# Keys turned before the query maxima, a ninth weight buffer, and maxima subtracted four chunks at a time

## The chip, the cores and the metric

The kernel runs on one core of one Trainium2 chip. A time is the device time of one execution in microseconds (us). The kernel before took 442.67 us, the median of three runs (442.42 to 442.70). The profile is of one further execution, which took 442.15 us. The profiler's span of that execution, from its first to its last instruction, is 440.3 us; the other 1.9 us lie around it.

## The reference

Two layers follow one another. The first is a linear attention with softmax-like features ("hedgehog"), for 8 batches, 8 heads, 576 positions and 64 channels a head:

```python
def phi(x):
    proj = np.einsum('bhsd,df->bhsf', x, w_phi)              # 64 -> 128 features
    proj = proj - np.max(np.abs(proj), axis=-1, keepdims=True)
    return np.concatenate([np.exp(proj), np.exp(-proj)], axis=-1)
q_p, k_p = (phi(q), phi(k))
kv = np.einsum('bhsf,bhsd->bhfd', k_p, v);  z = np.sum(k_p, axis=2)
x = np.einsum('bhsf,bhfd->bhsd', q_p, kv) / (np.einsum('bhsf,bhf->bhs', q_p, z)[..., None] + 1e-06)
```

The second takes x as (8, 576, 512), transforms it over the positions, mixes the channels of the first 64 frequencies, each with a complex 512x512 matrix of its own (w_r, w_i), transforms back and ends with a small channel layer:

```python
X = np.fft.rfft(x, axis=1)[:, :64]
Yr = Xr @ w_r[m] - Xi @ w_i[m];  Yi = Xr @ w_i[m] + Xi @ w_r[m]      # for each frequency m
u = x + np.fft.irfft(Y, n=576, axis=1)
out = u + np.maximum(u @ w_ch, 0.0)
```

The frequency matrices are 64 x 512 x 512 x 2 numbers in float32, 134 MB of the 163.6 MB that the core reads.

## The kernel before, in words

**Attention.** The work is cut into 16 units, each of two batches and two heads (`Unit`, four groups g of heads by four pairs bp of batches). A unit goes through stages that are spread over four turns of one loop (lines 490 to 557): in turn n, unit n+2 (called R) has its keys and queries turned by TensorE (`turn_k`, `turn_q`), unit n+1 (K) gets its maxima and the exponentials of its keys (`rows_k`, `rows_q`, `exp_k`), unit n (Q) gets the sums over keys, the query features and the result (`kv`, `cols_q`, `exp_q`, `num`), and unit n-1 (P) is transformed over positions (`freq`, `keep_x`).

The maximum over features must be subtracted from the query features. The query features are laid out with features in partitions and positions in columns, while the maxima are found in the other layout (`rows_q`, a VectorE reduce). So `shift_q` (line 214) splits each maximum into three bf16 parts (two VectorE subtracts), TensorE transposes them into `pt`, ScalarE copies that to `mT` (96 x 128), and `cols_q` (line 229) subtracts them inside the accumulation: after each product of 512 columns, `shifted` adds four products of 128 columns whose weights are one column of `minus`, broadcast; each picks the maxima of one chunk of 128 positions.

**Mixing.** The frequency matrices come as 64 transfers of 8 frequencies, a quarter of the input channels and one of the two parts, read as 2 MB of float32 and cast to 1 MB of bf16 on the way (`wload`). `mix` takes one of them in 8 products. Each group of four units adds its 16 (or 12) matrices to the queue `mixq`; `some(n)` takes n of them in the attention loop, and each, unless it lay in borrowed memory (`held`), asks with `next_w(1)` for the next transfer. 44 matrices are mixed in the loop, the last 20 in the loop at line 884.

**After attention.** The loop at line 884 does between two mixes what else can be done: the channel layer of x alone, and the inverse transform of the frequencies that are complete (`todo`, `fill`). When the last matrix is mixed, the rest of the inverse transform, the last sum and the 20 stores of the output follow (`Last`, lines 940 to 966).

**Order and buffers.** Each engine keeps program order (`InOrder`). All loads of keys, queries, values and matrices are issued by GpSimd (POOL), one behind the other; a load that must wait for its buffer holds all behind it. Matrices have 8 buffers of 8 KB a partition (pool `pw`, tag "wt", line 83), keys, queries and values 2 each (`pin`). Tiles named `one` share four PSUM banks in rotation, tiles named `two` two pairs of banks. In the last part `yall` and `yl`, the frequencies brought together, take buffers of "wt" too, and so do output tiles (`of`, `ofr`, `rx`); `zall` has memory of its own in `pb` (line 575). All three are written by small copies that SyncE (SP) and POOL issue.

All calls go through the helper at line 37, so the profile gives L37 for nearly all instructions, and the tiles' names tell them apart.

Of the kernel before, what the change touches and what calls it, by code (L numbers as in the profile page):

```python
# [43 lines left out]
def kernel(  # L44
# [14 lines left out]
    pe, dve, act = (InOrder(tc, e) for e in (nc.tensor, nc.vector, nc.scalar))  # L59
# [20 lines left out]

    XTb = [pers.tile([128, 2, 2, 2, 2, B_, 32], BF16, name=f"XT{i}") for i in range(2)]

    pw_cm = tc.tile_pool(name="pw", bufs=8)
    pw = pw_cm.__enter__()
    pin_cm = tc.tile_pool(name="pin", bufs=2)
    pin = pin_cm.__enter__()
# [1 line left out]
    pm = pm_cm.__enter__()  # L88
    m3s = [pm.tile([128, 3, 32], F32, name=f"m3{i}", bufs=1) for i in range(2)]
    minus = pm.tile([96, 32], BF16, name="minus", bufs=1)  # L90


    def load(t, src, g, bp, eng):
# [6 lines left out]
    class Unit:  # L100
# [36 lines left out]

        def turn_q(self, part):
            if part == 0:
                self.qT = pm.tile([128, 9, 128], BF16, name="qT", bufs=3)  # L140
                self.m3 = m3s[self.bp % 2]
            self.turn(self.qb, self.qT, False, part)

# [70 lines left out]
        def shift_q(self):  # L214

            high = self.m3.bitcast(BF16).rearrange("p t (n s) -> p t n s", s=2)[:, :, :, 1]
            for t in range(2):
                dve.tensor_tensor(out=self.m3[:, t + 1, 0:18], in0=self.m3[:, t, 0:18],
                                  in1=high[:, t, 0:18], op=ALU.subtract)
            pt = one([96, 128], BF16)  # L220
            pe.transpose(pt, high.rearrange("p t n -> p (t n)"), ident_b)
            self.mT = pm.tile([96, 128], BF16, name="mT")
            act.copy(self.mT, pt)

        def shifted(self, out, n, stop):
            pe.matmul(out, lhsT=minus[:, n:n + 1].to_broadcast([96, 128]), rhs=self.mT,
                      start=False, stop=stop)

        def cols_q(self, i):

            if i < 2:
                ps = two([128, 2, 4, 128])
                for c2 in range(2):
                    pe.matmul(
                        ps[:, c2].rearrange("p n s -> p (n s)"),
                        lhsT=w2blk[:, c2 * 128:(c2 + 1) * 128],
                        rhs=self.qT[:, 4 * i:4 * i + 4, :].rearrange("p n s -> p (n s)"),
                        start=True, stop=False,
                    )
                    for j in range(4):  # L240
                        self.shifted(ps[:, c2, j, :], 8 * i + 2 * j + c2, j == 3)
            else:
                ps = one([128, 2, 128])
                for h in range(2):
                    pe.matmul(ps[:, h, :], lhsT=w2blk[:, h * 128:(h + 1) * 128],
                              rhs=self.qT[:, 8, :], start=True, stop=False)
                    self.shifted(ps[:, h, :], 16 + h, True)
            self.pa = ps

        def exp_q(self, i):  # L250
# [131 lines left out]
    ident_f = scr[:, 2176:2304]  # L382
# [9 lines left out]
    mf = scr[:, 2112:2176]  # L392
# [8 lines left out]
    def sc(i):  # L401
# [21 lines left out]
    for t in range(3):  # L423
        r = slice(32 * t, 32 * t + 32)
        dve.tensor_scalar_mul(out=minus[r], in0=ident_f[r, r], scalar1=-1.0)

    def forward_table():

# [58 lines left out]
    def unit(i):  # L487
        return units[i] if 0 <= i < len(units) else None

    for n in range(-2, len(units) + 1):  # L490
        P, Q, K, R = (unit(n + i) for i in (-1, 0, 1, 2))
        X = 0 if n < 4 else 6 if n == 4 else 3
        if Q:
            Q.exp_q(0)
        if K:
            K.rows_k(0)
            K.exp_k(0)
        if Q:
            Q.weigh_v2()
            if unit(n + 2):  # L500
                unit(n + 2).load_v()
        if P:
            P.freq()
            P.keep_x()
            if P.bp == NP - 1:
                mixq += [key for key in order if key[0] == P.g and (P.g < 2 or key[1] < 12)]
            if n == 4:
                some(2)
        if Q:
            Q.cols_q(1)  # L510
            Q.exp_q(1)
        some(1 if X else 0)
        if K:
            K.rows_k(1)
            K.exp_k(1)
        if Q:
            Q.kv()
        if K:
            K.rows_q(0)
            K.rows_k(2)  # L520
            K.rows_q(2)
            K.rows_q(1)
# [361 lines left out]
    while mixq:  # L884
        key = mixq.pop(0)
        g, o, i = key[0], key[1] // 2, key[1] % 2
# [9 lines left out]
        n = -(-max(len(todo) - A, 0) // (left - 7)) if left > 7 else math.ceil(len(todo) / (left - 0.4)) if left else 0  # L896
        if g == NG - 1 and i == 1:
# [5 lines left out]
            pt = [bank([128, 2, 128], BF16) for h in range(2)]  # L903
# [94 lines left out]
```

## Time and profile before

| | before |
|---|---|
| median of 3 runs | 442.67 us (442.42 to 442.70) |
| profiled execution, its span | 442.15 us, 440.3 us |
| busy, share of the span | PE 76%, DVE 65%, ACT 64%, POOL 22% |
| moved by DMA | 99.57 MB as written, mean 226 GB/s |
| `mT<-one` copy on ACT, x16 | 0.262 us each |
| `two<-mT,minus`, 128 columns, x256 | 0.219 us each (overlapping) |
| weight loads of `minus`, x288 | 0.098 us each |
| a transfer of a matrix | 18.4 us (w_r), 18.6 us (w_i) from issue to landing, median |

PE is TensorE, PEld its weight loads, DVE VectorE, ACT ScalarE. Busy shares are of the whole span, over parts with different limits: attention runs to about 300 us, mixing alone to about 404 us, and the output to the end. DMA's bytes are counted as written, after the cast. [...] the landing comes later, and how much later tells what lies ahead of it in the queue.

### The profile page before, as it was taken

What the parts mean: (1) busy time and instruction counts of PE and PEld (TensorE: products, weight loads), DVE (VectorE), ACT (ScalarE), POOL (GpSimd) and SP (SyncE); (2) the same over time, 40 slices, a digit from 0 to 9 for tenths busy, and PEclk for the clock granted to TensorE, in tenths of its full rate; (3) what the DMA queues carried; (4) which work ended last, traced back from release to release, by engine and by line L of the source; (5) the groups of instructions that cost most, each with busy time, mean ns of one, the idle gap of its engine ahead of it and who ended that gap; (6) DMA issues with size and microseconds to landing.
All of it is one profiled execution on the core that took longest, in us unless ns stands there. A gap on an engine that the chain in (4) does not pass through costs nothing.

```text
span 440.3 us, 10505 instructions
## 1 busy us (share of the span) xinstructions
PE 335.4 (76%) x4395; PEld 219.8 (50%) x4439; DVE 285.7 (65%) x560; ACT 282.6 (64%) x494; POOL 96.9 (22%) x138
## 2 busy tenths in 40 slices
PE   2577587577877867768778677597679998999993
PEld 2356475454655656556557556474335544343320
DVE  4655765864658556787596576768864334777694
ACT  3595786866869668778587577752544442656682
POOL 7132031111402122223123121124002121010071
PEclk9986886978969888989699689879999999999997
DMA  7999999999999999999999999999999999997787
GB/s 165 237 210 211 237 212 237 234 216 264 210 212 237 239 236 218 197 237 210 239 210 238 214 236 238 212 212 213 212 216 222 219 222 223 212 219 159 240 363 305
DMA packets 51583, 99.57 MB, mean 226 GB/s; under 512 B 2512, under 2 KB 13648, under 8 KB 51536
## 3 DMA queue, kind: packets, MB, share of 16 engines
q0 software_dynamic: 45376, 86.45, 99.9%
q1 hardware_dynamic: 6160, 12.45, 8.0%
q8 instruction: 34, 0.56, 0.5%
q14 instruction: 13, 0.11, 0.1%
HBM read 163.64 MB, written 9.44 MB: 393 GB/s over the span
## 4 chain that ended last, share of the span: by engine, by line
PE 41%; DVE 24%; ACT 17%; DMA 8%; issue 8%; POOL 1%; ACTq 0%; DVEq 0%; POOLq 0%
PE one L37 18%; PE pt L37 10%; ACT AB L37 9%; PE two L37 8%; DVE m L37 7%; DMA wt<-in_moe_w_r_dram 7%; DVE mk L37 6%; PE pp L37 4%; ACT XT L37 3%; DVE xs L37 2%; DVE XT L37 2%; ACT AQ L37 2%; DMA qb<-in_q_dram 2%; ACT kT L37 1%; DVE yacc L37 1%
## 5 line engine op out<-in xcount | busy, mean ns | idle before, releaser
L37 ACT ACTIVATE AB<-two 128x1024 bf16<-128x1024 f32 x64 | 62.0, 1026 | 13.1 <-DVE mk L37 9.2
L37 ACT ACTIVATE AQ<-two 128x1024 bf16<-128x1024 f32 x64 | 62.6, 1043 | 3.3 <-PE two L37 3.2
L37 ACT CAST xw<-pt 128x512 bf16<-128x512 f32 x50 | 29.4, 588 | 34.4 <-PE pt L37 34.4
L37 DVE TENSOR_REDUCE mk<-two 128x8 f32<-128x1024 f32 x32 | 38.9, 1218 | 15.1 <-PE two L37 15.1
L37 DVE RECIPROCAL rd<-one 128x6 f32<-128x6 f32 x48 | 9.4, 195 | 59.9 <-PE one L37 59.9
L37 DVE TENSOR_REDUCE m<-two 128x8 f32<-128x1024 f32 x32 | 39.2, 1224 | 12.8 <-PE two L37 12.6
L37 DVE TENSOR_TENSOR va<-vn,ee 128x1152 bf16<-128x1152 f32 x32 | 41.9, 1353 | 0.0
L37 PE MATMUL pt<-wchb,xT 128*128 128x512 bf16 x127 | 34.0, 379 | 9.3 <-DVE xT L37 7.7
L37 ACT COPY kT<-one 128x512 bf16<-128x512 bf16 (+1 forms) x32 | 19.3, 640 | 32.7 <-PE one L37 32.6
L37 PEld LDWEIGHTS <-xs 128*128 128x128 bf16 x624 | 31.3, 102 | 12.2 <-issue 6.8
L37 PEld LDWEIGHTS <-minus 96*128 96x128 bf16 x288 | 28.3, 117 | 17.2 <-issue 12.4
L37 POOL DMA_DIRECT2D wt<-in_moe_w_i_dram x28 | 20.9, 747 | 70.5 <-PE one L37 39.0
L37 POOL DMA_DIRECT2D wt<-in_moe_w_r_dram x30 | 22.3, 745 | 64.0 <-PE one L37 34.7
L37 PE MATMUL two<-w2blk,qT 128*128 128x256 bf16 x128 | 20.6, 286 | 19.5 <-ACT AB L37 9.6
L37 PE MATMUL two<-mT,minus 96*128 96x128 bf16 x256 | 31.3, 258 | 3.8 <-issue 2.8
L37 PEld LDWEIGHTS <-qT 128*128 128x128 bf16 x144 | 14.2, 101 | 37.0 <-issue 34.4
L37 POOL DMA_DIRECT2D kb<-in_k_dram x16 | 11.5, 718 | 89.7 <-PE one L37 88.9
L37 PE MATMUL one<-kvz,AQ 128*128 128x65 bf16 x512 | 31.1, 223 | 0.0
L37 PE MATMUL one<-wt,XT 128*32 128x512 bf16 x304 | 26.2, 434 | 4.6 <-DVE XT L37 2.7
L37 PEld LDWEIGHTS <-AQ 128*128 128x128 bf16 x512 | 27.9, 119 | 1.6 <-issue 0.4
L37 PE MATMUL two<-w2blk,kT 128*128 128x256 bf16 x128 | 21.7, 300 | 8.4 <-ACT AB L37 8.4
L37 DVE TENSOR_TENSOR xs<-one,rd 128x384 bf16<-128x384 f32 x48 | 26.7, 557 | 1.6
(144 smaller groups left out, 707.4 us busy)
## 6 DMA issues: line engine op xcount, KB each, us to landing
wt<-in_moe_w_r_dram POOLq DMA_DIRECT2D x30, 1024.0 KB, 18.4
wt<-in_moe_w_i_dram POOLq DMA_DIRECT2D x28, 1024.0 KB, 18.6
vn<-in_v_dram POOLq DMA_DIRECT2D x15, 576.0 KB, 13.3
out_dram<-of SPq DMA_DIRECT2D x16, 512.0 KB, 3.1
kb<-in_k_dram POOLq DMA_DIRECT2D x16, 288.0 KB, 12.4
qb<-in_q_dram POOLq DMA_DIRECT2D x16, 288.0 KB, 12.5
xs<-in_moe_w_i_dram POOLq DMA_DIRECT2D x2, 1024.0 KB, 22.6
yacc<-in_moe_w_r_dram POOLq DMA_DIRECT2D x1, 1024.0 KB, 9.6
```

Source lines behind the costliest of these rows:

```text
L37: ins = f(*args, **kwargs)
```

## The change

1. In the loop, `turn_k(0)` of unit R (four transposes of keys) is put ahead of `shift_q` of unit K, and `turn_k(1)` (five) right behind it. Both stood behind `cols_q(0)`. The load of the next keys stays where it was on POOL.
2. `shift_q` makes `mT` four times as wide: VectorE multiplies the transposed maxima, repeated four times, by a mask `apart`, so that block j keeps the rows of chunk j alone. `cols_q` then subtracts the maxima of four chunks in one product of 512 columns. The ScalarE copy goes. `apart` and new columns of `minus` are made at the start, by seven VectorE instructions.
3. The matrices get a ninth buffer, and after turn 3 one more transfer is asked for. `qT` has 2 buffers in place of 3, `mT` 1 in place of 2, and `zall` moves from its own memory into a buffer of "wt".
4. In turn 4 the two mixes `some(2)` move from behind `keep_x` to behind `kv`.

```diff
-    pw_cm = tc.tile_pool(name="pw", bufs=8)
+    pw_cm = tc.tile_pool(name="pw", bufs=9)
...
+    apart = pm.tile([96, 4], BF16, name="apart", bufs=1)
...
-                self.qT = pm.tile([128, 9, 128], BF16, name="qT", bufs=3)
+                self.qT = pm.tile([128, 9, 128], BF16, name="qT", bufs=2)
...
-            self.mT = pm.tile([96, 128], BF16, name="mT")
-            act.copy(self.mT, pt)
+            self.mT = pm.tile([96, 4, 128], BF16, name="mT", bufs=1)
+            dve.tensor_tensor(out=self.mT, in0=pt.unsqueeze(1).to_broadcast([96, 4, 128]),
+                              in1=apart.unsqueeze(2).to_broadcast([96, 4, 128]), op=ALU.mult)
...
-                    for j in range(4):
-                        self.shifted(ps[:, c2, j, :], 8 * i + 2 * j + c2, j == 3)
+                    self.shifted(ps[:, c2].rearrange("p n s -> p (n s)"), 2 * i + c2,
+                                 self.mT.rearrange("p j s -> p (j s)"))
...
+    every = mf[0:96, 0:32]
+    for t in range(3):
+        r = slice(32 * t, 32 * t + 32)
+        dve.tensor_copy(every[r], ident_f[r, r])
+    dve.tensor_reduce(out=mf[0:96, 32:36], in_=every[:, 0:32].rearrange("p (a j c) -> p j a c", a=4, j=4), axis=AX.XY, op=ALU.add)
+    dve.tensor_copy(apart, mf[0:96, 32:36])
+    dve.tensor_reduce(out=mf[0:96, 32:36].rearrange("p (a c) -> p a c", a=2), in_=every[:, 0:16].rearrange("p (a j c) -> p a c j", a=2, j=4), axis=AX.X, op=ALU.add)
+    dve.tensor_scalar_mul(out=minus[:, 0:4], in0=mf[0:96, 32:36], scalar1=-1.0)
...
-            if n == 4:
-                some(2)
...
+        some(2 if n == 4 else 0)
...
+        if R:
+            R.turn_k(0)
         if K:
             K.shift_q()
+        if R:
+            R.turn_k(1)
         if Q:
             Q.num(0)
         if K:
             K.cols_q(0)
-        if R:
-            R.turn_k(0)
-            R.turn_k(1)
-            if unit(n + 4):
-                unit(n + 4).load_k()
+        if R and unit(n + 4):
+            unit(n + 4).load_k()
...
+        elif n == 3:
+            next_w(1)
...
-    zall = pb.tile([128, B_, DMODEL], BF16, name="zall", bufs=1)
+    zall = pw.tile([128, B_, DMODEL], BF16, name="zall", tag="wt")
```

More of the change, by code (lines that the diff above doesn't have):

```diff
@@ L221, in shift_q, with shifted @@
             pe.transpose(pt, high.rearrange("p t n -> p (t n)"), ident_b)
-            self.mT = pm.tile([96, 128], BF16, name="mT")
-            act.copy(self.mT, pt)
-        def shifted(self, out, n, stop):
-            pe.matmul(out, lhsT=minus[:, n:n + 1].to_broadcast([96, 128]), rhs=self.mT,
-                      start=False, stop=stop)
+            self.mT = pm.tile([96, 4, 128], BF16, name="mT", bufs=1)
+            dve.tensor_tensor(out=self.mT, in0=pt.unsqueeze(1).to_broadcast([96, 4, 128]),
+                              in1=apart.unsqueeze(2).to_broadcast([96, 4, 128]), op=ALU.mult)
+        def shifted(self, out, n, rhs):
+            pe.matmul(out, lhsT=minus[:, n:n + 1].to_broadcast([96, 128]), rhs=rhs,
+                      start=False, stop=True)
         def cols_q(self, i):
@@ L246, in cols_q @@
                               rhs=self.qT[:, 8, :], start=True, stop=False)
-                    self.shifted(ps[:, h, :], 16 + h, True)
+                    self.shifted(ps[:, h, :], 16 + h, self.mT[:, 0, :])
             self.pa = ps
@@ L425 @@
         dve.tensor_scalar_mul(out=minus[r], in0=ident_f[r, r], scalar1=-1.0)
+    every = mf[0:96, 0:32]
+    for t in range(3):
+        r = slice(32 * t, 32 * t + 32)
+        dve.tensor_copy(every[r], ident_f[r, r])
+    dve.tensor_reduce(out=mf[0:96, 32:36],
+                      in_=every[:, 0:32].rearrange("p (a j c) -> p j a c", a=4, j=4),
+                      axis=AX.XY, op=ALU.add)
+    dve.tensor_copy(apart, mf[0:96, 32:36])
+    dve.tensor_reduce(out=mf[0:96, 32:36].rearrange("p (a c) -> p a c", a=2),
+                      in_=every[:, 0:16].rearrange("p (a j c) -> p a c j", a=2, j=4),
+                      axis=AX.X, op=ALU.add)
+    dve.tensor_scalar_mul(out=minus[:, 0:4], in0=mf[0:96, 32:36], scalar1=-1.0)
     def forward_table():
```

## The prediction

> **What bounds the kernel now.** I read the page's slices and queues first.
>
> ```profile
> span 440.3 us, 10505 instructions
> ...
> DMA  7999999999999999999999999999999999997787
> GB/s 165 237 210 211 237 212 237 234 216 264 210 212 237 239 236 218 197 237 210 239 210 238 214 236 238 212 212 213 212 216 222 219 222 223 212 219 159 240 363 305
> ...
> q0 software_dynamic: 45376, 86.45, 99.9%
> ```
>
> No engine is near 100%, but the DMA engines are over 90% in every slice from 11 to 396 us, and the packets of POOL's queue q0 fill 99.9% of sixteen engines' time (they overlap, so that sum alone proves little). The question is whether this is a full pipe or only a long wait in it. The DMA view of single issues, asked for short windows at 179, 302 and 369 us, decides (last column: us from issue to landing).
>
> ```profile
> wt<-in_moe_w_i_dram POOLq DMA_DIRECT2D x1, 1024.0 KB, 9.9
> ...
> wt<-in_moe_w_r_dram POOLq DMA_DIRECT2D x1, 1024.0 KB, 32.2
> wt<-in_moe_w_i_dram POOLq DMA_DIRECT2D x1, 1024.0 KB, 37.6
> ...
> wt<-in_moe_w_i_dram POOLq DMA_DIRECT2D x1, 1024.0 KB, 35.2
> ```
>
> With POOL's issue times these give landings. The matrices issued at 295.66, 297.94, 300.15 and 300.94 us land at 313.2, 318.0, 323.1 and 328.0: 4.95 us apart, whatever the distance of their issues. The last, issued at 369.06, lands at 404.3, after 35.2 us, 30 of them behind six others. So the matrices come as fast as the queue gives them, and one that is asked for earlier only stands in the queue longer.
>
> Then the timeline, for who waits for whom near the end (start, us, engine, operation; idle time in brackets).
>
> ```profile
> 368.09 0.20 PEld L37 LDWEIGHTS <-XT 128*32 128x32 bf16 x8 [0.89 <-DMA wt<-in_moe_w_r_dram]
> ...
> 404.56 0.66 PE L37 MATMUL pt<-wt,XT 128*32 128x512 bf16 x8
> ...
> 415.92 1.22 DVE L37 TENSOR_TENSOR of<-pp,rl 128x1024 f32<-128x1024 f32 x1 [0.48 <-DMA out_dram<-of]
> ```
>
> At 368 us TensorE waits for a matrix; from there on it works nearly without a gap and meets the last one 0.3 us after its landing. The two run abreast: DMA needs 36.2 us from 368.05 to 404.3, TensorE 36.5 from 368.09 to 404.56. The 36 us after that need the last matrix and are fixed. The chain of waits names PE 41% and DMA only 8%; it follows a load back to the mix that freed its buffer, and so hides that the queue itself is the limit.
>
> Before 300 us attention does not follow DMA: at 282.8 us TensorE mixes a matrix that landed 28 us earlier (issued at 236.9, 18.1 us to landing). Its last mix in the loop starts at 300.5 us, 2.4 us after its matrix landed (283.72 + 14.4 = 298.1). That 2.4 us is all that a faster attention can hand on.
>
> **What the Trainium skill says.** "DMA: Bandwidth & Descriptors", section "Where 436 GB/s comes from", puts the ceiling of a core's SBUF ports at 435 GB/s. A matrix reads 2.097 MB in 4.95 us: 424 GB/s, so the trace agrees and the pipe is full. The same page, "Issuing engines are not separate DMA queues", says that transfers of all issuers share 16 engines: between 328 and 368 us, where SP's copies of `yst` and `zst` run, matrices land 5.2 to 6.2 us apart. "VectorE: DVE Perf Modes", "The perf-mode tier table", gives `tensor_tensor` with a PSUM operand the plain rate; the rows here agree (128x512 in 0.69 us, 128x384 in 0.56).
>
> **Part by part.** *Keys ahead of the maxima.* One turn before (69 to 74 us):
>
> ```profile
> 69.93 0.34 PE L37 MATMUL one<-ident_b,m 128*96 128x128 bf16 x1 [1.51 <-DVE m L37]
> ...
> 70.31 0.26 ACT L37 COPY mT<-one 96x128 bf16<-96x128 bf16 x1 [0.46 <-PE one L37]
> ...
> 72.43 1.17 PE L37 MATMUL one<-ident_b,kb 128*128 128x128 bf16 x9
> ```
>
> Four of nine transposes, 4/9 x 1.17 = 0.52 us, fall into the wait of 1.51. But the banks of `one` rotate by four: in the turns with mixing (n from 4 on) the running sum of `mix` takes one, and `turn_k(0)` must wait for the bank that `exp_k(2)` reads. At 195 us that read ends at 195.94, while the maxima's transpose started at 195.47 after a wait of 0.26. There it starts 0.5 (bank) + 0.5 (four transposes) - 0.1 = about 0.9 us later, and what is moved forward is only given back behind it. So: +0.5 us a turn for the six early turns, 0 for the later (between -0.9 and +0.5). POOL: the load of keys can be issued up to 2 us earlier; that only lengthens its stay in the queue.
>
> *Wide mT.* VectorE gains 16 x about 0.65 us (between the 0.56 and 0.69 rows), ScalarE loses 16 x 0.262. `mT` is ready 0.4 us later, covered by `turn_k(1)` (0.65) and `num(0)` (0.87), which stand ahead of its reader; without this cover 0.4 a turn. TensorE: two groups of four 128-column products take 0.43 us each at 71 us, where a product of 512 columns takes 0.42: gain 0. At 61 us the eight take 0.83, where two of 512 would take 0.42: 0.4 gained, beside a wait for ScalarE. I take 0.4 a turn on the path, between 0 and 0.8. The start gets seven VectorE instructions (copies of 32x32 like the 0.17 of `minus`, small reduces), about 1.5 us, while the queue holds over 10 us of loads.
>
> Attention in sum: 6 x 0.5 + 16 x 0.4 - 1.5 = about +8 us, from -8 (6 x 0.5 - 11 x 0.9 - 1.5) to +14. Of a gain, 2.4 us reach the mixing loop, and there TensorE meets the DMA wait of 368 us earlier. At the end: 0.
>
> *Ninth buffer and the extra load.* Bytes, their order at the end and the stores are the same, so 404.3 moves only where the pipe ran thin. There is one such place; DMA's rate from 170 to 190 us in half-us slices:
>
> ```profile
> GB/s 213 204 213 205 208 208 203 175 171 230 283 359 249 280 177 174 160 184 139 147 201 201 205 217 168 205 184 197 217 221 201 213 213 217 228 190 200 199 207 207
> ```
>
> At 172.9 us the queue holds only 3.8 us of work (the loads before it land by 176.7). Against about 208: six slices from 177 us at a mean of 163.5 lose 0.64 us, two at 173.5 lose 0.17, four from 182 lose 0.19; together 1.0. The landings agree: 5.8 and 5.2 us for two matrices, 1.2 over. With one more matrix ahead the queue has 3.8 + 4.95 us there: gain 1.0, between 0.4 and 1.3. The extra load goes ahead of the values of unit 6, issued at 98.15 and landed after 9.9 us; with 5 more they use 15 of the 34 us until they are read. `some(2)` behind `kv` delays one matrix load by about 5 us, with 8 + 5 us of queue as cover.
>
> *Places.* `qT` with 2 and `mT` with 1: their last readers come before the writers in the same turn; 0. `zall` in "wt": in the mixing loop 9 - 2 buffers in place of 8 - 1 (`yl` is first written at 386 us, when all loads are issued); 0. It is free before the output, so there one more buffer stands ready, and the 0.48 us wait of `of` at 415.92 goes; TensorE ran half beside it: 0.2 gained (0 to 0.4).
>
> Sum: 1.0 + 0.2 = 1.2 us. The profiled execution would take 442.15 - 1.2 = 441.0; it is 0.5 below the median, so the median comes to 442.67 - 1.2 = 441.5.
>
> **Rivals.** *Nothing at all.* The thin place is one of many small losses, another arises, or the queue gets no deeper because the new loads wait elsewhere on POOL: 442.4 to 442.9. For it: other matrices land 0.3 to 0.8 us late in a full queue (118.6 us, 271.6). Against: the rate falls only where the queue is short.
>
> *Attention's gain comes through.* 8 us off: 434. For it: 25.6 us of TensorE's weight loads wait for the maxima. Against: TensorE would have to mix matrices before they land.
>
> *The bank of `exp_k(2)`.* In the eleven late turns the maxima come 0.9 us later and nothing is gained back: 10 us lost and 1.5 at the start, 3 gained early. Attention then ends 8 us late; TensorE has 0.9 us in hand at 368, so the end comes 7 us later: 449.8. It decides as soon as attention ends more than 0.9 us later than before. For it: the wait of 0.26 leaves no room. Against: four transposes fewer stand between the maxima and `num(6)`, and only the sum counts there.
>
> **How the numbers follow.** Pipe refilled 0.68 (440.6 to 442.3), nothing 0.16, gain through 0.03, bank 0.13 (443.6 to 452). A measurement can tell about 0.2% from no change: below 441.8 is faster, above 443.55 slower. Three quarters of the first case (0.51) and the third give faster 0.54; the rest of the first and the second give same 0.33; slower 0.13. The range leaves out the third case, the last and a few hundredths of the first: 440.3 to 443.6.
>
> **What would show it.** Right: the last matrix lands at about 403.3 us, the rate near 175 us stays above 200 GB/s, the wait of `of` is gone, 36 us follow the last mix, and attention ends earlier than 300.5 us with longer landings. Wrong: a last mix that starts well after its landing (attention or mixing became the bound), an empty q0, values landing after 32 us, or a tail that is not 36 us.

## The result, and the profile after

| | before | after |
|---|---|---|
| median | 442.69 us (442.42 to 443.00, 4 runs) | 442.92 us (441.78 to 443.16, 4 runs) |
| ratio of the two | | 1.0000 (95%: 0.9981 to 1.0019) |
| profiled execution, its span | 442.15 us, 440.3 us | 443.16 us, 441.4 us |
| last matrix lands | 404.27 us | 404.06 us |
| last mix starts | 404.56 us | 405.24 us |
| from there to the span's end | 35.7 us | 36.1 us |

With four executions on each side nothing is seen. Two later comparisons, with more executions, give 441.06 us against 441.87 (0.9988, 95%: 0.9978 to 0.9997) and 441.40 against 441.80 (0.9986, 0.9976 to 0.9995). The medians differ by 0.8 and 0.4 us, and both intervals leave out 1 (the ratios are the record's own and not the quotients of the medians). So there is a gain, of about 0.13%. The first comparison, uncertain by 0.19%, could not have shown it.

The page of the changed kernel, with the same rows as were shown of the one before:

```profile
span 441.4 us, 10119 instructions
...
DMA  8999999999999999999999999999999999995787
GB/s 164 237 211 210 237 212 237 235 214 242 233 211 238 223 230 232 237 216 233 232 216 235 208 236 231 219 212 211 211 216 223 221 224 215 213 218 127 243 354 305
...
q0 software_dynamic: 45376, 86.45, 99.6%
...
DMA 39%; PE 30%; DVE 12%; ACT 9%; issue 7%; POOL 0%; ACTq 0%; POOLq 0%; DVEq 0%
```

Slices and queue are as full as before. The one slice that was low, 197 GB/s in the 17th, reads 237. The chain of waits has turned round, DMA 39% where it was 8%, though the limit is the same. Attention now arrives early and waits for matrices, so the chain meets the transfers that it formerly passed by.

The rate in half-us slices from 170 to 190 us, asked of DMA as before:

```profile
GB/s 225 205 209 201 225 217 205 201 221 254 188 191 207 221 200 206 202 247 290 299 285 255 294 312 290 241 193 213 209 221 201 209 217 225 197 209 217 221 205 202
```

No slice is below 188, where eight were at or below 177 before. The thin place, the stretch in which the queue had little work left and the rate fell, is gone. The last matrix is issued at 369.95 us; the DMA view of that issue has it land 34.1 us later.

```profile
wt<-in_moe_w_i_dram POOLq DMA_DIRECT2D x1, 1024.0 KB, 34.1
```

So the pipe was refilled, and in this execution its end came 0.2 us sooner, not 1.0. From there to the last mix it took 0.9 us longer, and from the last mix to the end 0.4 us longer. The 0.4 are taken up with the single parts below; for the 0.9 TensorE's timeline tells where (start, us, engine, operation; idle time in brackets):

```profile
362.17 0.66 PE L37 MATMUL pt<-wt,XT 128*32 128x512 bf16 x8 [1.31 <-DMA wt<-in_moe_w_i_dram]
...
364.16 1.80 PE L37 MATMUL pt<-wchb,yT 128*128 128x256 bf16 x8 [0.19 <-ACT yT L37]
...
368.98 0.66 PE L37 MATMUL pt<-wt,XT 128*32 128x512 bf16 x8
...
405.24 0.66 PE L37 MATMUL pt<-wt,XT 128*32 128x512 bf16 x8
```

At 362.17 it has waited 1.31 us for a matrix. Then eight products of 256 columns take 1.80 us, and the next mix starts 6.81 us after this one; before, the two were 5.62 us apart (362.47 and 368.09). The windows of six us show the granted clock (next to the DMA share, third from the end). First the kernel before:

```profile
362.00:368.00 6.00, 4.87 (x38) 2.42 (x37) 2.37 (x7) 2.27 (x6) 0.74 (x1) 1.00 1.13 220
```

and the changed one:

```profile
362.00:368.00 6.00, 4.85 (x31) 2.78 (x32) 1.84 (x5) 0.74 (x2) 0.74 (x1) 0.72 1.11 214
```

The mean of 0.72 is half the clock for about 3.4 us of these six. TensorE is busy as long (4.85 us) and does 31 products in place of 38. From 368 us on it has no time in hand, so the 1.2 us are still there at the last mix, 1.18 us after the landing.

In the last part, VectorE's timeline has the addition that was to win 0.2 us:

```profile
416.60 1.22 DVE L37 TENSOR_TENSOR of<-pp,rl 128x1024 f32<-128x1024 f32 x1 [0.48 <-PE pp L37]
```

Its wait is as long as before, 0.48 us, and now for TensorE.

### The profile page after: what moved, and what is told of

It reads as the page before. It is cut to its first block, busy times and chain, and to the rows that moved or that the text cites. A ratio compares the mean times of both kernels' runs of the same rounds, so it can differ in the third digit from the quotient of the medians.

```text
span 441.4 us, 10119 instructions
## 1 busy us (share of the span) xinstructions
PE 330.6 (75%) x4203; PEld 201.8 (46%) x4247; DVE 298.0 (68%) x583; ACT 278.3 (63%) x478; POOL 97.2 (22%) x138
## 4 chain that ended last, share of the span: by engine, by line
DMA 39%; PE 30%; DVE 12%; ACT 9%; issue 7%; POOL 0%; ACTq 0%; POOLq 0%; DVEq 0%
DMA vn<-in_v_dram 18%; PE one L37 11%; DMA wt<-in_moe_w_r_dram 9%; PE pt L37 9%; DMA wt<-in_moe_w_i_dram 6%; ACT AB L37 5%; PE pp L37 5%; PE two L37 5%; DMA kb<-in_k_dram 5%; DVE mk L37 3%; DVE m L37 2%; DVE xs L37 2%; DMA qb<-in_q_dram 2%; ACT AQ L37 1%; DVE va L37 1%
## 5 line engine op out<-in xcount | busy, mean ns | idle before, releaser
L37 DVE TENSOR_REDUCE m<-two 128x8 f32<-128x1024 f32 x32 | 39.2, 1224 | 15.3 <-PE two L37 15.2
L37 PE MATMUL pt<-wchb,xT 128*128 128x512 bf16 x127 | 35.1, 389 | 8.1 <-DVE xT L37 6.3
L37 PE MATMUL one<-wt,XT 128*32 128x512 bf16 x304 | 27.8, 451 | 13.9 <-DMA wt<-in_moe_w_i_dram 5.6
L37 PE MATMUL two<-w2blk,qT 128*128 128x256 bf16 x128 | 22.8, 309 | 18.2 <-ACT AB L37 9.7
L37 ACT COPY qT<-one 128x512 bf16<-128x512 bf16 (+1 forms) x32 | 19.3, 641 | 26.2 <-PE one L37 25.8
L37 PEld LDWEIGHTS <-XT 128*32 128x32 bf16 x512 | 14.4, 149 | 33.9 <-issue 18.8
L37 PE MATMUL two<-mT,minus 96*128 96x512 bf16 x64 | 27.1, 424 | 3.5 <-issue 1.5
L37 PEld LDWEIGHTS <-AQ 128*128 128x128 bf16 x512 | 24.2, 107 | 7.7 <-issue 3.9
L37 PE MATMUL one<-kvz,AQ 128*128 128x65 bf16 x512 | 26.9, 207 | 1.1 <-ACT qT L37 1.0
L37 PE MATMUL one<-va,AB 64*128 64x65 bf16 x1024 | 22.9, 199 | 4.1 <-DVE va L37 4.0
```

Source lines behind the costliest of these rows:

```text
L37: ins = f(*args, **kwargs)
```

## The experiments

Medians of one comparison share the executions of the kernel before on the same chip. Where a profile is compared, it is one execution, and its place among the others is told where it matters.

### The changed kernel once more, and each part alone

The first runs the changed kernel unchanged.

> The changed kernel once more. Theory 1 (the last matrix lands when the slowest DMA engine has done its share, and that engine never ran dry before the change either): the last matrix lands at 404.1 us within 0.4; the end is 36 us behind the last mix. Where TensorE's granted clock does not fall in the stretch from 355 to 375 us, the last mix follows its landing by 0.3 to 0.6 us; where it falls again, by about 1.2. Median 442.3 to 443.1. Rival (the thin place refilled is worth 1.0 us and was lost by chance in the profiled execution): landing near 403.3, median near 441.7.

The keys' order alone, on the kernel before:

```diff
+        if R:
+            R.turn_k(0)
         if K:
             K.shift_q()
+        if R:
+            R.turn_k(1)
...
-        if R:
-            R.turn_k(0)
-            R.turn_k(1)
-            if unit(n + 4):
-                unit(n + 4).load_k()
+        if R and unit(n + 4):
+            unit(n + 4).load_k()
```

> Only the order of the key transposes. Theory 1: same time as before within 0.2%, last matrix at 404.2 us, although attention ends earlier; I expect the mix of matrix 40 of the loop's 44 (the one that starts at 299.2 us before and at 286.5 after the whole change) 3 to 6 us earlier. Rival (the bank that the key transposes wait for delays the maxima in the turns with mixing): that mix starts later than 299 us and the time rises by as much.

The wide `mT` alone, with its mask and the start's seven instructions:

```diff
+    apart = pm.tile([96, 4], BF16, name="apart", bufs=1)
...
-            self.mT = pm.tile([96, 128], BF16, name="mT")
-            act.copy(self.mT, pt)
+            self.mT = pm.tile([96, 4, 128], BF16, name="mT", bufs=1)
+            dve.tensor_tensor(out=self.mT, in0=pt.unsqueeze(1).to_broadcast([96, 4, 128]),
+                              in1=apart.unsqueeze(2).to_broadcast([96, 4, 128]), op=ALU.mult)
...
-                    for j in range(4):
-                        self.shifted(ps[:, c2, j, :], 8 * i + 2 * j + c2, j == 3)
+                    self.shifted(ps[:, c2].rearrange("p n s -> p (n s)"), 2 * i + c2,
+                                 self.mT.rearrange("p j s -> p (j s)"))
```

> Only the wide mT with one product for four chunks. Theory 1: same time within 0.2%; the mix that starts at 299.2 us before comes 6 to 9 us earlier (0.4 us a turn were expected). Rival (VectorE's multiply delays the query features): later than 299 us, and the time rises by as much.

The ninth buffer alone, with its load and the place that `qT` and `zall` give it:

```diff
-    pw_cm = tc.tile_pool(name="pw", bufs=8)
+    pw_cm = tc.tile_pool(name="pw", bufs=9)
...
-                self.qT = pm.tile([128, 9, 128], BF16, name="qT", bufs=3)
+                self.qT = pm.tile([128, 9, 128], BF16, name="qT", bufs=2)
...
+        elif n == 3:
+            next_w(1)
...
-    zall = pb.tile([128, B_, DMODEL], BF16, name="zall", bufs=1)
+    zall = pw.tile([128, B_, DMODEL], BF16, name="zall", tag="wt")
```

> Only the ninth buffer, with the extra load and the moves that make room. Theory 1: the thin place near 175 us is gone, the first of the sixteen DMA engines finishes each late matrix about 1 us earlier than before, the last of them not; last landing 404.2 us within 0.3, time the same, the mix at 299.2 us unmoved. Rival (the pipe as a whole was short): last landing near 403.3 us and a time 1.0 us shorter.

Measured, beside 441.87 us for the kernel before (59 runs):

| | median, us | ratio (95%) | least work in the queue, 100 to 300 us | last turn starts at |
|---|---|---|---|---|
| before | 441.87 | | 3.8 us | 284.88 us |
| all parts | 441.06 | 0.9988 (0.9978 to 0.9997) | 16.9 us | 270.75 us |
| keys alone | 442.00 | 1.0006 (0.9997 to 1.0014) | 12.8 us | 273.11 us |
| wide `mT` alone | 442.38 | 1.0012 (1.0002 to 1.0022) | 6.9 us | 279.50 us |
| ninth buffer alone | 441.54 | 0.9995 (0.9987 to 1.0003) | 12.5 us | 280.39 us |

"Least work in the queue" is the smallest time from an issue of POOL to the landing of what was issued ahead of it; "last turn" is the last transpose of maxima, `one<-ident_b,m`. Both are from one profile each, for the kernel before from its first. Item 4 of the change, the two mixes moved in turn 4, was not run alone. Each part alone takes the thin place away, since an earlier attention asks for matrices earlier just as a ninth buffer does. In the three profiles the last matrix lands 0.5 to 0.8 us sooner than before (403.73, 403.47 and 403.75 us, against 404.26 in the mean of two). The medians don't follow: no part alone is clearly faster than the kernel before, and only all parts together are. So what the refilled place alone is worth in time is not shown.

Of what was expected, the changed kernel was to land its last matrix at 404.1 us within 0.4 and to take 442.3 to 443.1. It landed it at 403.04 and took 441.06, which is nearer to the rival named there. The mix that starts at 299.18 us before comes 11.6 us earlier with the keys' order alone (3 to 6 were expected), 6.2 with the wide `mT` (6 to 9) and 4.5 with the ninth buffer (none).

Those 4.5 us need not come from the buffer. The stretch from the second to the third transpose of maxima, on the kernel before and with the ninth buffer alone (after the length: busy time of PE, PEld, DVE, ACT and POOL; then the granted clock):

```profile
35.30:52.70 17.40, 12.39 (x203) 10.34 (x206) 11.40 (x20) 12.92 (x22) 3.61 (x5) 0.79 1.14 211
34.50:49.40 14.90, 10.46 (x204) 8.42 (x204) 11.40 (x20) 12.42 (x22) 3.61 (x5) 0.93 1.14 210
```

VectorE and POOL are busy for the same time, TensorE for 1.9 us less at a higher clock, and the turn is 2.5 us shorter. From the seventh transpose of maxima to the last the two kernels' turns agree within 0.1 us. The changed kernel by itself does the same turn in 14.5 us (two profiles, clock 1.00) and in 16.3 (one, 0.81). The short turns go with the higher clock; which of them is the cause is not shown. The time of attention in one profile is therefore certain only to a few us.

The wide `mT` alone is slower in the median by 0.5 us, and its profile has a candidate for the cause in the output. The seventh store is issued 14.9 us behind the last mix in every profile. In the kernel before, with the wide `mT` alone and in the first profile of all parts it takes (last column):

```profile
out_dram<-of SPq DMA_DIRECT2D x1, 512.0 KB, 3.0
...
out_dram<-of SPq DMA_DIRECT2D x1, 512.0 KB, 4.8
...
out_dram<-of SPq DMA_DIRECT2D x1, 512.0 KB, 4.9
```

VectorE's eleventh addition of the output, in the same three:

```profile
423.41 1.22 DVE L37 TENSOR_TENSOR of<-pp,rl 128x1024 f32<-128x1024 f32 x1 [0.27 <-PE pp L37]
...
423.96 1.23 DVE L37 TENSOR_TENSOR of<-pp,rl 128x1024 f32<-128x1024 f32 x1 [1.21 <-PE pp L37]
...
424.10 1.23 DVE L37 TENSOR_TENSOR of<-pp,rl 128x1024 f32<-128x1024 f32 x1 [0.27 <-issue]
```

With eight buffers it starts 0.1 us after that store has landed (19.68 and 19.80 us behind the last mix), 0.94 us later than before, and the end comes 36.7 us behind the last mix in place of 35.7. The profile names TensorE for this wait, but its products `pp` had been done for about a microsecond. With nine buffers the store lands as late (19.81) and the addition does not wait (18.86). In all eight profiles with the wide `mT` the seventh store takes 3.8 to 5.1 us, and a fetch of instructions, 16 KB on queue q8, starts 15.3 to 16.3 us behind the last mix. In the six without it the store takes 3.0 us and the fetch starts at 3.2 to 3.6. That the fetch delays the store is therefore likely, but it was not tried. The same stores end the first profile of all parts 0.4 us later; in its second profile they are late too and cost nothing.

In the keys' order alone, the timeline answers the question of the bank at the place where the prediction had asked it (a turn with mixing):

```profile
185.70 0.67 ACT L37 ACTIVATE ABr<-one 128x256 bf16<-128x256 f32 x2
...
186.00 0.61 PE L37 MATMUL one<-ident_b,kb 128*128 128x128 bf16 x4
...
186.40 0.32 PE L37 MATMUL one<-ident_b,m 128*96 128x128 bf16 x1
...
186.51 0.74 PE L37 MATMUL one<-ident_b,kb 128*128 128x128 bf16 x5
```

The keys' transposes begin at 186.00 us, while the read `ABr` of `exp_k(2)` ends at 186.37. They do not wait for it, and the maxima follow 0.40 us behind them. In all fifteen turns of this profile in which keys are turned, they begin 0.36 to 1.51 us before that read ends. Where they wait for a bank at all (0.2 us, in three turns), it is for the read `AQr` of `exp_q(2)`. The sixth maxima transpose comes 5.7 us earlier than before (103.46 and 109.15 us). From it to the sixteenth, ten turns, this kernel needs 169.65 us where the kernel before needs 175.7, which would be 0.6 us a turn. The three profiles of all parts need 174.8, 167.4 and 173.1 us for the same turns, so the size of the late gain is not certain; that nothing is lost there is seen in all four.

### With half the bytes: what attention gains by itself

Each transfer fetches only the first of each two rows of a matrix, and both products of a pair use it. Half of each matrix is left out, so these two kernels don't compute the reference; their instructions are otherwise the same.

```diff
-            wt.rearrange("p m r e -> p m (r e)"),
+            wt[:, :, 0, :],
...
-                "m (p r) e -> p m (r e)", r=2))
+                "m (p r) e -> p m r e", r=2)[:, :, 0, :])
...
-                    rhs=wt[:, j, r, :], start=(first and r == 0), stop=(last and r == 1),
+                    rhs=wt[:, j, 0, :], start=(first and r == 0), stop=(last and r == 1),
```

> The kernel before with half of each matrix left out: each transfer brings the first of two rows alone and mix uses it twice, so engines do the same work and DMA moves 33 MB less as written. Theory 1 (DMA sets the time of both kernels): with the load gone, compute sets it; the time falls well below 442 us, to about 410 to 432.

> The changed kernel with the same half of each matrix left out. Theory 1: the gain of attention, which cannot pass while matrices are late, passes here: 9 to 14 us below the light kernel before. Rival (the mixing loop gives the gain back by itself, DMA or not): within 2 us of it.

Beside 442.18 us for the kernel before they take 438.16 us (0.9888, 95%: 0.9847 to 0.9930) and 426.15 us (0.9637, 0.9604 to 0.9670). From the page and the timeline of the lighter kernel before:

```profile
span 433.2 us, 10550 instructions
...
GB/s 167 233 207 201 130 165 153 147 112 97 149 183 184 124 143 138 149 183 191 121 174 189 89 146 102 94 146 190 141 38 133 148 167 162 2 73 10 245 364 304
```

```profile
397.49 0.66 PE L37 MATMUL pt<-wt,XT 128*32 128x512 bf16 x8
```

and of the lighter changed kernel:

```profile
span 421.4 us, 10163 instructions
...
GB/s 165 234 206 206 163 173 172 146 138 170 205 169 139 166 140 150 180 150 174 170 152 158 98 149 109 70 181 197 108 37 135 139 182 109 16 60 25 262 359 302
```

```profile
385.55 0.66 PE L37 MATMUL pt<-wt,XT 128*32 128x512 bf16 x8
```

The rate has holes everywhere, so the transfers no longer set the end (in the first, the last matrix lands 29 us before its mix). Then the change is worth 12.0 us, in the median, the span (11.8) and the last mix (11.9) alike. So the change does speed attention up, by more than the 8 us of the prediction. With the full bytes nearly all of it turns into waiting for matrices.

The pair also shows how near the kernel before was to a balance. From the mix of (3, 0) to the last mix TensorE needs 98.7 us in the lighter changed kernel (286.82 to 385.55), where it waits for no matrix. The kernel before needs the same 98.7 with all bytes (305.87 to 404.56). It was bound by TensorE and DMA at once. (The lighter kernel before needs 99.8, but has half its clock from 302.44 to 309.27 us.)

### Attention slowed in both

The reduce of the last two query chunks (`rows_q(2)`) is done twice, 0.41 us of VectorE a unit, 6.6 us in all.

```diff
-            dve.tensor_reduce(out=out, in_=src, axis=AX.X, op=ALU.max,
-                              apply_absolute_value=True)
+            for _ in range(2 if tT is getattr(self, "qT", None) and i == 2 else 1):
+                dve.tensor_reduce(out=out, in_=src, axis=AX.X, op=ALU.max,
+                                  apply_absolute_value=True)
```

> The kernel before with the reduce of the last two query chunks done twice: 0.41 us more on VectorE in each of 16 units, nothing left out. Theory 1 with TensorE abreast of DMA (0.9 us in hand at 368 us): attention ends up to 6.6 us later and the time rises by 3 to 6 us. Rival (DMA alone sets the time, compute has room): same as before.

> The changed kernel with the same doubled reduce. Theory 1: its attention has about 12 us in hand, so the 6.6 us cost nothing: within 0.3% of the changed kernel. Rival (no real gain in attention): it rises by 3 to 6 us too.

Beside the same 442.18 us the slowed kernel before takes 447.71 us (1.0115, 95%: 1.0083 to 1.0148), the slowed changed one 442.45 us (1.0007, 0.9995 to 1.0019). TensorE's last mixes in the attention loop, in the slowed kernel before:

```profile
305.91 1.96 PE L37 MATMUL one<-wt,XT 128*32 128x512 bf16 x32
```

and in the slowed changed kernel:

```profile
293.19 1.08 PE L37 MATMUL one<-wt,XT 128*32 128x512 bf16 x8 [4.59 <-DMA wt<-in_moe_w_r_dram]
298.15 1.08 PE L37 MATMUL one<-wt,XT 128*32 128x512 bf16 x8 [3.87 <-DMA wt<-in_moe_w_i_dram]
```

Of 6.6 us the kernel before passes 5.5 on (3.7 to 6.5 by the interval). It mixes four matrices in a row without a wait at 305.91, so they had been there: attention is what is late. The transfers follow it, for they are asked for later. The queue has about 1 us of work left at 176 us, the rate falls to 5 GB/s in one half-us slice there, and the last matrix lands at 409.38 us, 1.2 us before its mix. The changed kernel swallows all of it: it still has 4.59 and 3.87 us of waiting to give away. This is what the change bought: a reserve in attention of more than 6.6 us that this kernel has no use for. It also prices the rival in which attention ends late: 6.6 us late cost 5.5, as "8 us late, 7 at the end" had it. Only the premise failed.

### The clock of TensorE

Five products of 512 columns of the identity, into a bank that nobody reads, fill the time before the mix of (3, 11); beside it the changed kernel once more.

```diff
+        if key == (3, 11):
+            warm = bank()
+            for w in range(5):
+                pe.matmul(warm, lhsT=ident_b, rhs=wchb[:, 0, :], start=(w == 0), stop=(w == 4))
         mix(*key, wts.pop(key), XTb[g % 2], bank)
```

> The changed kernel with five products of 512 columns (identity by the output weights, into a bank that nobody reads) ahead of the mix of matrix (3, 11), before which TensorE waited 1.31 us for DMA at 362 us in the profile after. They add no bytes and, if TensorE waits there anyway, no time. Theory (TensorE, made to wait by an early attention, is sometimes given half its clock for 3.4 us just where it has no time in hand, about 1 us at the end): no half-clock interval between 355 and 375 us, the last mix at most 0.4 us after the last landing, and a median 0.2 to 0.6 us below that of the changed kernel beside it. Rival (the clock's halving is set by something else than this wait, or costs nothing on most executions): no difference beyond 0.2 us, or 0.3 to 1 us longer if the five products come when the matrix is already there.

> The changed kernel once more, as the measure for the kernel with the five products. If the half clock near 365 us comes in about a third of executions: median within 0.3 us of the kernel before or up to 0.6 us below it, last landing 403.0 to 404.1 us in the profile, last mix 0.2 to 1.2 us after it.

With the five products 441.35 us (440.69 to 442.11, 21 runs; 0.9987, 95%: 0.9980 to 0.9994), without 441.40 (440.71 to 442.78, 22 runs; 0.9986, 0.9976 to 0.9995), both beside 441.80. A median 0.2 to 0.6 us lower had been expected; it is 0.05 lower. The profiles show windows of 3.4 us, ahead of the place in question and behind it. The changed kernel of the first comparison:

```profile
360.90:364.30 3.40, 1.37 (x14) 0.58 (x15) 1.04 (x3) 0.95 (x2) 0.74 (x1) 1.00 1.12 223
364.30:367.70 3.40, 3.18 (x15) 2.01 (x15) 0.80 (x3) 0.37 (x1) 0.00 (x0) 0.50 1.11 201
```

The changed kernel run here, where the clock falls at 363.69:

```profile
360.29:363.69 3.40, 1.26 (x13) 0.53 (x12) 0.85 (x3) 0.96 (x2) 0.74 (x1) 1.00 1.12 223
363.69:367.09 3.40, 3.13 (x14) 2.06 (x16) 0.99 (x3) 0.37 (x1) 0.00 (x0) 0.50 1.12 211
```

The changed kernel beside the single parts:

```profile
360.90:364.30 3.40, 1.98 (x20) 1.18 (x20) 1.05 (x3) 0.96 (x2) 0.74 (x1) 1.00 1.12 223
364.30:367.70 3.40, 3.40 (x32) 1.83 (x31) 1.18 (x3) 1.54 (x3) 0.00 (x0) 1.00 1.12 217
```

The five products, as TensorE's timeline has them (it holds four of the five):

```profile
360.97 1.24 PE L37 MATMUL pt<-wchb,ident_b 128*128 128x512 bf16 x4
362.15 0.66 PE L37 MATMUL pt<-wt,XT 128*32 128x512 bf16 x8
```

Where TensorE was busy 1.37 and 1.26 us of the first window, it has half its clock in the second (0.50), and with 1.98 it has all of it. Of eleven profiles with full bytes and the mix at this time, the slowed changed kernel's, with 1.58, is the third that lost its clock; the eight others had 1.98 to 2.81 us (the five products 2.58) and kept it. The same holds elsewhere. The changes of clock in a trace lie on a grid of 3.41 us, and these windows can be counted from 20 to 405 us in the twelve profiles with full bytes. At full clock, every window with less than 1.55 us of busy TensorE was followed by one at half clock, and none with more than 1.96 us was; in between there were both. "TensorE: Matmul & The Clock Gate", section "Part 1: The HAM clock gate", of the Trainium skill knows such a gate with two states, full and half, set over windows of about 3.4 us. The length and the half agree. It gives one idle window as the condition for the fall; here TensorE was not idle for a whole window at this place, and being busy for less than half of one was enough.

The three profiles with the fall have their last mix 1.18, 1.24 and 1.19 us after the last landing, the other eight 0.04 to 0.83. So it costs about 0.4 to 1.1 us in such an execution, but that it sets the median is not seen. The profile of the changed kernel run here is the slowest of its 22 executions (442.78). With the fall made away with, the median is 0.05 us lower, which is nothing, and the slowest execution 442.11. So the fall explains most of what the first profile after lost, and perhaps the upper end of the executions. In the median the rival is right: the fall costs nothing that could be measured.

### The thin place made again, and the kernel before once more

In the changed kernel four loads are kept back in the turns n = 8 and 9 (`TA` is 8), and issued together behind the load of keys of turn 9.

```diff
-                    next_w(1)
+                    if (turn[0] == TA and len(skip) > 0) or (turn[0] == TA + 1 and not released):
+                        saved.append(key)
+                    else:
+                        next_w(1)
...
+        if n == TA + 1:
+            released.append(1)
+            next_w(len(saved))
```

> The changed kernel with four loads of matrices held back from 169 to 186 us and issued together at about 189 us, behind a load of keys, so that the queue runs down to about 3.8 us of work there, as it did before the change at 172.9 us. Nothing else is changed, and no matrix comes late for its mix (they are mixed about 30 us after they land). Theory A (the slowest of the 16 DMA engines sets each landing; a thin place idles the others and lets the slowest catch up): the spread of the 16 signals, 2.8 us before the place, falls by 1 us or more there; at the last matrix the first of the 16 comes at 399.8 or later (397.9 to 398.9 in the changed kernel without the hold), the last at 403.0 to 404.3, at most 0.6 us later than without; median within 0.6 us of the kernel before. Theory B (what the sum of all engines loses there is lost at the end, the reading of the prediction): all 16 come about 1.0 us later, 1st 399.4 and last 404.6, the spread stays above 5; median about 1.0 us above the changed kernel's, 0.4 us or more above the kernel before.

> The kernel before once more, for a second profile of it: how much its last landing and the spread of the 16 engines differ from one execution to the next. If the first profile was typical: thin place at 170 to 190 us again, spread falling there from about 2.8 to below 1.8 us, last landing 403.9 to 404.7, last mix at most 0.6 us after it, and a wait of `of` for its buffer of about 0.5 us at 416 us. If it was not: a last landing at or below 403.6, in which case the ninth buffer gained less than 0.3 us.

The first gives 441.60 us (0.9998, 95%: 0.9986 to 1.0009; before 441.86), and does not decide. POOL's timeline shows why:

```profile
185.05 0.71 POOL L37 DMA_DIRECT2D kb<-in_k_dram  x1 [6.44 <-PE one L37]
185.75 0.74 POOL L37 DMA_DIRECT2D wt<-in_moe_w_r_dram  x1
```

The keys could be loaded at 185.05 us, some 4 us earlier than I had reckoned, and what was issued ahead landed at 193.5. So the queue never held less than 8.5 us of work and no thin place arose. What is seen is that one matrix can be asked for 17.7 us later and three 4 to 7 us later (185.75 to 188.26 us, against 168.00 to 183.87 in the second profile of all parts) at no cost to the end: the last lands at 402.95 us. In this run, depth beyond what kept the queue from running dry was worth nothing.

The second profile of the kernel before is like the first: again 3.8 us of work at the least, at 172.6 us, the last landing at 404.24 and the last mix at 404.49. Two things differ. The rate from 170 to 190 us falls less, with four slices at or below 177 in place of eight, though the last matrix lands at the same time:

```profile
GB/s 213 211 213 199 204 212 202 166 194 249 260 380 334 300 222 205 229 205 205 209 225 205 160 180 168 217 180 188 205 176 205 209 180 202 189 196 208 198 207 204
```

The other is on VectorE's timeline:

```profile
415.85 1.23 DVE L37 TENSOR_TENSOR of<-pp,rl 128x1024 f32<-128x1024 f32 x1 [0.49 <-PE pp L37]
```

The same addition waits as long, and for TensorE. In the first profile the store that was named had landed at the same moment; TensorE alone makes the wait as long.

### Sixteen engines, read one by one

"DMA: Bandwidth & Descriptors", section "Why a DMA increments its semaphore by 16 and not by 1", says that a transfer runs on up to 16 engines that finish independently, and that only all 16 signals mean that the data is there. The trace holds these signals. For the last matrix they came as follows (us from the span's start; mix is TensorE's start of the last mix, lag its distance from the last signal; these are worked out from the trace's signals, as no view of the profile lists them):

```
                            1st      8th     16th     mix     lag
before                    400.41   402.57   404.27   404.56   0.29
before, second profile    399.73   402.53   404.24   404.49   0.25
all parts, first          398.85   401.51   404.06   405.24   1.18
all parts, second         397.92   400.79   403.04   403.30   0.26
all parts, third          397.70   400.79   403.50   404.75   1.24
with five products        397.83   401.01   403.78   403.88   0.10
four loads kept back      397.60   400.78   402.95   403.77   0.83
keys alone                397.51   400.68   403.73   403.77   0.04
wide mT alone             397.73   401.09   403.47   404.16   0.69
ninth buffer alone        397.62   400.58   403.75   403.79   0.04
```

Early in the kernel, from 14 us on, the first and last signal of a transfer are 0.7 to 1.0 us apart. The distance grows, to 2.6 to 2.8 us at 173 us in the kernel before, and to 5.1 to 5.8 at the end in the three profiles of all parts (6.2 with the keys' order alone). In the kernel before it falls in the thin place, from 2.78 to 1.57 us (second profile: 2.59 to 1.73), and so it does in the slowed kernel before (2.44 to 1.62). The reading that fits is that the fast engines have nothing to do there while the slow ones work off what they had; the signals don't tell which engine sent them.

By this reading the thin place cost the fast engines most. In the means of two profiles before and three of all parts, filling it brings the first signal 1.9 us sooner, the eighth 1.5, and the last 0.7 (404.26 to 403.53; single ones 0.2 to 1.2). The three executions of all parts are not typical ones: one had the longest time of its four, one the shortest of 14, one the longest of 22. TensorE waits for the last signal. That the spread falls in a thin place is seen in the three profiles that have one. A run that makes the place again and nothing else is missing, and why an engine is slow stays open. The 34 fetches of instructions of 16 KB (a mean of 0.95 us each in the kernel before) are one candidate, but nothing was tried that would prove it.

## Why the prediction was right or wrong

**The bound** was right. DMA's queue and TensorE ran abreast, and an attention that ends 10.8 to 14.1 us earlier moved the median by less than 1. The two pairs of runs show both sides of the balance. One argument for it was not sound: the 424 GB/s are counted as read. After the cast half as many bytes, 212 GB/s, enter SBUF, so they say little beside a ceiling of its ports. What shows the full queue is that matrices land 4.95 us apart whatever the distance of their issues.

**Keys ahead of the maxima.** "+0.5 us a turn for the six early turns, 0 for the later" was too low in the one profile of this part: 5.7 us in the early turns in place of 3, and 0.6 a turn in the late ones. How much of that belongs to the clock is open, since the ninth buffer alone gains 4.1 us in the same early turns. The step that failed is "`turn_k(0)` must wait for the bank that `exp_k(2)` reads": in the trace it starts before that read ends, in every turn. I had inferred the bank from the rotation and not from a wait in the trace, where there was none to read.

**Wide `mT`.** 0.4 us a turn less 1.5 at the start makes 4.9; alone it moved the last turn by 5.4. It agrees, within the few us by which one profile of attention is uncertain. The 0.5 us that the median of this kernel loses (1.0012) was not foreseen; its profile loses 0.94 us to a late store and a buffer that is not free.

**Attention in sum.** +8 (-8 to +14) was 12.0 in the lighter pair. That it is worth 0 at the end fits the median of the keys' order alone (1.0006). An earlier attention fills the thin place as the buffer does, which the prediction had not seen, so the two don't add up.

**Ninth buffer.** The step "gain 1.0, between 0.4 and 1.3" has the right place and sign for the last landing, and its term was mis-sized: 0.7 in the mean of all parts, 0.2 to 1.2 singly, 0.5 with the buffer alone. It was read from the rate summed over 16 engines, and TensorE waits for the last of them. In time the buffer alone gives 0.9995 (0.9987 to 1.0003), which can't be told from nothing.

**`of`.** "The 0.48 us wait of `of` at 415.92 goes" was wrong, and the 0.2 us there are 0: TensorE's products make the wait just as long. One more buffer before the output is of use, but at another place and only where a store is late. There it saves the 0.94 us that the wide `mT` alone loses.

**What was left out.** An earlier attention makes TensorE wait for DMA just ahead of the stretch in which it has nothing in hand, and in three of eleven profiles it lost half its clock there. The prediction did name the DMA wait that TensorE would meet earlier, and gave it no price; its own sign of being wrong, "a last mix that starts well after its landing", came with it. It is 0.4 to 1.1 us in the executions that have it, two of the three profiles of all parts among them. That the wide `mT` goes with later stores was left out as well; it costs up to 0.6 us behind the last mix even with nine buffers (36.1, 35.7 and 36.2 us in the three profiles).

**The sum.** 1.2 us were expected, and "faster" was held likelier than "same" (0.54 to 0.33). 0.4 and 0.8 came in the medians of the two longer comparisons, none in the first, short one, and all of them lie within 0.2% of no change. The measured 442.92 us lies inside the stated 440.3 to 443.6, but so does no change at all, and part of it is luck: a gain of 12 us in attention where 8 were reckoned, and a bank that nobody waits for, did not count because the bound held. Of the rivals, "nothing at all" describes what the first comparison sees, and in part for its reason: other losses did arise, the half clock and the later stores, though not in the queue, which got deeper (16.9 us at the least). "Attention's gain comes through" would have been right by 12 us with half the bytes. "The bank" had the price right and a premise that the trace refutes.

## What to carry to other kernels

Where a queue is full, ask first what a change can be worth at most: in these profiles a refilled thin place brought the last signal 0.7 us sooner, where the rate had promised 1.0, and several edits that fill the same place don't add up. Prove a gain off the critical path by lightening the bound (half the bytes here), and the balance by slowing the suspect; two pairs of runs told more than all single parts, whose effects of 0.1% hardly stand out. When work is made to wait for a transfer, look at the granted clock behind the wait. And look at the part of the kernel that the change does not touch: here its stores became later.

## What was not expected of the hardware

- The 16 signals of one transfer drift apart, from 0.7 to 1.0 us between first and last early on to 5.1 to 5.8 us after 400 us of full load with all parts, and close up where the queue runs thin.
- At full clock, between 20 and 405 us, TensorE's clock fell to half for the next 3.41 us after every window in which TensorE was busy for less than 1.55 us of 3.41, and after none with more than 1.96 us.
- The seventh store took 3.8 to 5.1 us in the eight profiles in which a fetch of instructions started 0.4 to 1.5 us behind its issue, and 3.0 us in the six in which it did not.
- A chain of waits that names DMA with 8% and with 39% can belong to kernels with the same limit and times within 0.2% of each other.
